# Two buffers for key-query loads, shifted keys and the middle block, kept sums in DRAM, and attention pairs traced four steps apart

## The chip, the cores and the metric

The kernel runs on one core of a Trainium2 chip. The metric is the device time of one execution in microseconds (us); lower is better. The core's engines are TensorE (PE, with its weight loads as PEld), VectorE (DVE), ScalarE (ACT), GpSimd (POOL) and SyncE (SP), which here only issues DMAs. Each engine works through its own list of instructions in order.

## The reference

```python
def phi(x):
    proj = np.einsum('bhsd,df->bhsf', x, w_phi)
    proj = proj - np.max(np.abs(proj), axis=-1, keepdims=True)
    return np.concatenate([np.exp(proj), np.exp(-proj)], axis=-1)
q_p, k_p = (phi(q), phi(k))                       # batch 4, heads 8, seq 576, head_dim 64, 128 features
kv = np.einsum('bhsf,bhsd->bhfd', k_p, v)
z = np.sum(k_p, axis=2)
num = np.einsum('bhsf,bhfd->bhsd', q_p, kv)
den = np.einsum('bhsf,bhf->bhs', q_p, z)[..., None] + 1e-06
x = num / den                                     # reshaped to 2304 tokens x 512
h = x @ w_in                                      # 512 x 2048, weights given in 64 bits
g = np.where(h > 0.0, h, np.exp(np.minimum(h, 0.0)) - 1.0)
x = g @ w_out                                     # 2048 x 512
for e in range(4):                                # second layer: 4 experts of 512 x 1024 x 512
    out += p[:, e:e + 1] * (np.maximum(x @ w1[e], 0.0) @ w2[e])
```

## The kernel before

The work has three stages that overlap in the order in which the engines get it.

**Attention.** The 32 heads are worked on two at a time: 16 pairs, each a Python generator `pair(i)`. One pair does the following. It projects keys and queries with `w_phi` (L209 for the middle block of 64 keys and 64 queries, L192 sixteen times: eight for the keys, eight for the queries). DVE takes the largest absolute value of each row (L198) and subtracts it (L199, into `md`, `kp` and `qd`). ACT exponentiates the shifted keys (L202, L203). PE transposes the shifted queries (L238, L256), and ACT exponentiates them on their way out of PSUM (L246, into `ew`). PE multiplies keys with values (L231, L232: the keys are the stationary operand, the values the moving one), where the tile `vt` holds 64 columns of values and 64 columns of ones, so that the sum over keys comes out with the product. ACT copies that product out of PSUM (L260, `kvw`). PE then computes the denominator (L295) and the numerator (L285) from `kvw` and `ew`. The reciprocal goes through DRAM to be spread over partitions (L309, L313), DVE multiplies (L316), and ACT and POOL split the result into two parts `xh` and `xl`, the input of the next stage.

**First layer ("Elu").** 2304 tokens are 9 tiles of 256; the hidden dimension's first half is 4 units `u`. `Elu.l1` makes 24 matmuls (L483 to L485) of 128x256, `Elu.l2` makes 24 more (L512 to L514), two units later. The first two tiles are done in two halves (`SEG`), so their sum after unit 1 is kept until unit 3 (`drain`). The weights arrive as 64-bit words and are converted by `convert64`: a DMA (L108), two ACT steps (L116, L117), four DVE steps (L120 to L123), POOL steps (L125, L127), and a split (L132, L134). `CVL` is how many conversions are loaded ahead of the `CVB` = 4 that are being worked on; the pool has `CVB + CVL` buffers for them.

**The rest**, from about 455 us on, is the second half of the first layer and the four experts, in a Strassen form (L610 to L612, L712 to L714).

Attention is traced step by step: `attention()` starts a new pair every `ATT_LAG` steps and advances each live pair by one yield per step. The Elu units are traced between, and a scheduler in the compiler then orders all instructions of all engines by its own model, so that the constants below act through the order it finds. `load(i + 1)` issues a pair's loads of keys, queries and values; `kq` has `LDB` buffers, `vt` two by hand.

Of the kernel before, what the change touches and what calls it, by code (L numbers as in the profile page):

```python
# [8 lines left out]
F32 = mybir.dt.float32  # L9
# [4 lines left out]
ALU = mybir.AluOpType  # L14
# [3 lines left out]
B, H, S, D, FEAT = 4, 8, 576, 64, 128  # L18
NT, DM, DFF, E, F2 = 2304, 512, 2048, 4, 1024
P = 128  # L20
KD = DM // P
NP = H // 2
HS = S // 2
Q = 32
TS = 256
# [15 lines left out]
WL = 'G'  # L41
LAG = 2
RING = 16
ATT_LAG = 5
PRE = 1.2
RATE = 1.4
WRATE = 2
WHEAD = 5
CVB = 4
CVL = 2  # L50
TAIL = 2
HEAD = 2
SEG = 2
# [3 lines left out]
CB = 2  # L57
TEB = 2
PB = 4
LDB = 1  # L60
CVP = 16
CVW = 256
CVOFF = 0
# [5 lines left out]
def attn_elu_moe_kernel(ctx: ExitStack, tc: tile.TileContext, kq_in, vv, w_phi, w_in, w_out, probs, w1, w2, out):  # L69
    nc = tc.nc  # L70
    V, A, G, PE, SP = nc.vector, nc.scalar, nc.gpsimd, nc.tensor, nc.sync
# [5 lines left out]
    def pool(name, bufs=1, stack=ctx, **kw):  # L77
        return stack.enter_context(tc.tile_pool(name=name, bufs=bufs, reuse_waits="tile", **kw))

    const = pool("const")  # L80
    dram = ctx.enter_context(tc.tile_pool(name="dram", bufs=1, space=bass.MemoryType.DRAM))
# [4 lines left out]
    xvd = [[dram.tile([P, 2, 2, TC], F32, name=f"xvd{g}_{k}") for k in range(7)] for g in range(NG)]  # L86
    rscr = [dram.tile([2, S], F32, name=f"rec{i}") for i in range(B * NP)]
    x1scr = [dram.tile([P, KD, TS], F32, name=f"x1scr{t}") for t in range(NTS)]
    ring = pool("ring", RING)
    pst = ExitStack()  # L90
    psum = [pool("psum", 7, space=PSUM, stack=pst)]
# [14 lines left out]
    def convert64(dst, src, adder):  # L106
        st = cv.tile([P, CVW], I64, tag="w64", name="w64", bufs=CVB + CVL)
        SP.dma_start(st, src)  # L108
# [29 lines left out]
    tmp = pool("tmp", stack=right, side="right")  # L138
    gt = pool("gt", LAG + 1, stack=right, side="right")
    ld = pool("ld", LDB, stack=att)  # L140
    a1 = pool("a1", stack=att)
    wbd = a1.tile([P, 2, FEAT], F32, name="wbd")
    ident = a1.tile([P, P], F32, name="ident")
    vt = []

    def load(i):
        b, p = divmod(i, NP)
        kq = ld.tile([P, 2 * S], F32, tag="kq", name="kq")
        SP.dma_start(kq[:, :640], kq_in[b, p, :, :640])
        if i == 0:  # L150
            SP.dma_start(wbd, w_phi)
        SP.dma_start(kq[:, 640:], kq_in[b, p, :, 640:])
        v = vt[i % 2]
        SP.dma_start(v[:, 0:4, 0:D], vv[b, p, :, 0:4, :])
        SP.dma_start(v[:, 4:8, D:P], vv[b, p, :, 4:8, :])
        SP.dma_start(v[0:D, 8, 0:D], vv[b, p, 0:D, 8, :])
        SP.dma_start(v[0:D, 9, D:P], vv[b, p, D:P, 8, :])
        return kq, v

    def bank(shape=(P, 512)):  # L160
        return psum[0].tile(list(shape), F32, tag="bank", name="bank")
# [7 lines left out]

    make_identity(nc, ident)  # L170
    for i in range(2):
        t = a1.tile([P, 10, P], F32, name=f"vt{i}")
        G.memset(t, 1.0)
        vt.append(t)
    kpm = a1.tile([P, 2, 2, P], F32, name="kpm")
    G.memset(kpm, 0.0)
    loaded = {0: load(0)}

    def blocks(t, n):
        return t[:, :n * P].rearrange("p (n f) -> p n f", f=P)  # L180

    def pair(i):
        b, p = divmod(i, NP)
        kq, v = loaded.pop(i)
        kt, qt = kq[:, :512], kq[:, 640:]

        def proj(src):
            ps = [bank() for _ in range(2)]
            for t in range(4):
                for h in range(2):  # L190
                    r = slice(h * D, h * D + D)
                    PE.matmul(blocks(ps[h], 4)[:, t], src[r, t * P:(t + 1) * P], wbd[r, h], start=True, stop=True)  # L192
            return ps

        def guard(dst, ps, n):
            src = blocks(ps, n)
            mx = a1.tile([P, n, 1], F32, tag=f"mx{n}", name="mx", bufs=2)
            V.tensor_reduce(out=mx[:, :, 0], in_=src, op=ALU.max, axis=AX.X, apply_absolute_value=True)  # L198
            mark[0] = V.tensor_tensor(out=dst, in0=src, in1=mx.to_broadcast([P, n, P]), op=ALU.subtract).ins  # L199

        def kexp(d0, d1, src):
            A.activation(d0, src, ACTF.Exp)  # L202
            A.activation(d1, src, ACTF.Exp, scale=-1.0)  # L203

        kp = [a1.tile([P, 4, 2, P], F32, tag=f"kp{j}", name=f"kp{j}") for j in range(2)]
        md = a1.tile([P, 2, P], F32, tag="md", name="md")
        qd = [a1.tile([P, 4, P], F32, tag=f"qd{j}", name=f"qd{j}") for j in range(2)]
        pm = bank()
        PE.matmul(pm[:, :2 * FEAT], kq[:, 512:640], wbd, start=True, stop=True)  # L209
# [7 lines left out]
        yield  # L217
        kexp(kpm[:D, :, 0], kpm[:D, :, 1], md[:D])
        kexp(kp[1][:, :, 0], kp[1][:, :, 1], kp[1][:, :, 1])
        pq0, pq1 = proj(qt)  # L220
        guard(qd[0], pq0, 4)
        if i + 1 < B * NP:
            loaded[i + 1] = load(i + 1)
        yield
        guard(qd[1], pq1, 4)
        yield
        pk = bank((P, 4, P))

        def kv(h, c):
            for t in range(4):  # L230
# [3 lines left out]
        def tpose(j):  # L234
            pt = bank()
            for t in range(2):
                for h in range(2):
                    PE.transpose(blocks(pt, 4)[:, 2 * h + t], qd[h][:, 2 * j + t], ident)  # L238
            return pt

        ew = a1.tile([P, 2, 2, S], F32, tag=("eh", "el")[i % 2], name="ew")

        def qexp(ps, c0, n):
            src = ps[:, :512].rearrange("p (h s) -> p h s", h=2)[:, :, :n] if n > P else blocks(ps, 2)[:, :, P - n:]
            for c, sc in ((0, 1.0), (1, -1.0)):
                A.activation(ew[:, :, c, c0:c0 + n], src, ACTF.Exp, scale=sc)  # L246

        kvw = a1.tile([P, 4, P], F32, tag=("kvh", "kvl")[i % 2], name="kvw")
        qexp(tpose(0), 0, 256)
        kv(0, 0)  # L250
        kv(0, 1)
# [25 lines left out]
        def half(s):  # L277
            return slice(s * HS, (s + 1) * HS)

        def num(s):  # L280
            pn = bank()
            for c in range(2):
                for h in range(2):
                    r = slice(h * D, h * D + D)
                    PE.matmul(pn[r, :HS], kvw[:, 2 * h + c, r], ew[:, h, c, half(s)], start=(c == 0), stop=(c == 1))  # L285
            A.activation(nd[:, half(s)], pn[:, :HS], ACTF.Copy)

        def den():
            pd = bank()
            for c in range(2):  # L290
                for h in range(2):
                    for s in range(2):
                        g = (2 * h + s) * Q
                        ones = D - h * D
                        PE.matmul(pd[g:g + Q, :HS], kvw[:, 2 * h + c, ones:ones + Q], ew[:, h, c, half(s)], start=(c == 0), stop=(c == 1))  # L295
            A.activation(dd, pd[:, :HS], ACTF.Copy)

        dd = a1.tile([P, HS], F32, tag="dd", name="dd")
# [20 lines left out]
    done = [0]  # L319

    def attention():
# [3 lines left out]
        while nxt < B * NP or live:  # L325
            if nxt < B * NP and step % ATT_LAG == 0:
                live.append(pair(nxt))
# [62 lines left out]
    def weight_stream():  # L390
# [3 lines left out]
        while more or loaded or live:  # L394
            if more and len(loaded) < CVL:
                g = next(todo, "end")
                if g == "end":
                    more = False
                else:
                    next(g[0])  # L400
                    loaded.append(g)
            if loaded and len(live) < CVB and (len(loaded) == CVL or not more):
                live.append(loaded.pop(0))
# [59 lines left out]
            next(weights, None)  # L463

    stream = attention()
    accs, saved = {}, {}
    HU = FP // 2
    count = [0]

    class Elu:  # L470
# [28 lines left out]

        def l2(self, slot):  # L500
            key = self.t
            if self.first:
                accs[key] = [bank((P, 2, TS)) for a in range(2)]
            acc = accs[key]
            for j in range(2):
                w = rings["out", 2 * self.u + j]
                for dc in range(KD):
                    c = slice(dc * P, (dc + 1) * P)
                    o = acc[dc // 2][:, dc % 2]
                    start = self.first and j == 0 and dc % 2 == 0  # L510
                    stop = self.last and j == 1 and dc % 2 == 1
                    PE.matmul(o, w[:, 0, c], self.gh[:, j], start=start, stop=False)  # L512
                    PE.matmul(o, w[:, 0, c], self.gl[:, j], start=False, stop=False)  # L513
                    PE.matmul(o, w[:, 1, c], self.gh[:, j], start=False, stop=stop)  # L514
                if j == 0:
                    slot()
            if self.last:
                self.drain(acc)
            if self.t == NTS - 1:
                release(("out", 2 * self.u), ("out", 2 * self.u + 1))  # L520
            slot()

        def drain(self, acc):
            done = self.u == HU - 1
            for a in range(2):
                st = (tmp if done else a1).tile([P, 2, TS], F32, tag="xs" if done else "xp", name="xs", bufs=2 if done else 2 * HEAD)
                if (self.t, a) in saved:
                    V.tensor_tensor(out=st, in0=acc[a], in1=saved[self.t, a], op=ALU.add)
                else:
                    A.activation(st, acc[a], ACTF.Copy)  # L530
                if done:
                    A.dma_start(x1scr[self.t][:, 2 * a:2 * a + 2], st)
                else:
                    saved[self.t, a] = st

    def pieces(i, size):
        o = 0
# [426 lines left out]
```

## Time and profile before

| | |
|---|---|
| median of three runs | 1411.74 us (1411.62 to 1415.79) |
| the profiled execution, its device time | 1409.39 us |
| span of the profiled execution, first to last instruction | 1407.6 us |
| PE busy | 1361.3 us, 97% of the span |
| DVE, ACT, POOL busy | 664.9, 601.5, 361.1 us |
| mean granted TensorE clock | 0.992 of full speed |

Busy time is the union of an engine's instructions; what is left of the span is idle. The granted clock is the share of TensorE's clock that it was given: 1.00 is 2.4 GHz, 0.50 is 1.2 GHz. PE is busy nearly all the time, so the question for any stage is when PE waits there, and for whom.

### The profile page before, as it was taken

The numbers are of one execution on the slowest core, as the hardware profiler recorded it, in microseconds if no ns is written. First come the engines' busy times: TensorE is split into PE (matmuls) and PEld (weight loads), VectorE is DVE, ScalarE is ACT, GpSimd is POOL, SyncE is SP. The second block draws the span as 40 slices with busy tenths as digits, with TensorE's granted clock in tenths as the row PEclk, the third lists the DMA queues.
The fourth block names the chain that finished last, engine by engine and source line by source line (L and its number), as shares of the span: only waits on it lengthen the run. The fifth ranks groups of instructions, "written<-read, shape, count | busy, mean of one in ns | idle before, by whom it ended". The sixth has DMA issues, their size and how long they took to land.

```text
span 1407.6 us, 22023 instructions
## 1 busy us (share of the span) xinstructions
PE 1361.3 (97%) x8408; PEld 1234.4 (88%) x8408; DVE 664.9 (47%) x1212; ACT 601.5 (43%) x1347; POOL 361.1 (26%) x433
## 2 busy tenths in 40 slices
PE   6799899999999999999999999999999999999998
PEld 6678778888999899999898989888888989889897
DVE  5677766564443666684433423324433325323232
ACT  5667755554545646573333442123421214321121
POOL 3457644221226211263202440002420004300000
PEclk9999989999999999999999999999999999999999
DMA  5434455431324130446425142434145351433521
GB/s 160 135 121 143 130 178 157 138 111 46 116 78 128 42 118 29 128 167 208 155 92 207 37 156 91 157 115 148 53 150 209 103 175 45 142 120 128 179 68 68
DMA packets 105337, 173.46 MB, mean 123 GB/s; under 512 B 33040, under 2 KB 50576, under 8 KB 105232
## 3 DMA queue, kind: packets, MB, share of 16 engines
q1 hardware_dynamic: 98224, 162.55, 35.5%
q10 hardware_dynamic: 7008, 9.51, 1.9%
q8 instruction: 66, 1.08, 0.3%
q14 instruction: 39, 0.32, 0.1%
HBM read 118.13 MB, written 53.81 MB: 122 GB/s over the span
## 4 chain that ended last, share of the span: by engine, by line
PE 69%; DMA 5%; issue 3%; POOL 3%; DVE 3%; ACT 2%; SPq 0%; ACTq 0%; DVEq 0%; POOLq 0%
PE bank L610 9%; PE bank L612 9%; PE bank L611 9%; PE bank L712 9%; PE bank L713 9%; PE bank L714 9%; PE bank L689 2%; PE bank L690 2%; PE bank L691 2%; DMA w<-in_w_out 2%; POOL w L443 1%; DMA wst<-in_w 1%; PE bank L483 1%; PE bank L512 1%; PE bank L485 1%
## 5 line engine op out<-in xcount | busy, mean ns | idle before, releaser
L610 PE MATMUL bank<-xv,w 128*128 128x384 f32 x840 | 278.5, 336 | 4.8 <-DVE c L661 2.6
L611 PE MATMUL bank<-xv,w 128*128 128x384 f32 x840 | 281.8, 335 | 0.0
L612 PE MATMUL bank<-xv,w 128*128 128x384 f32 x840 | 277.8, 335 | 0.0
L713 PE MATMUL bank<-w,h 128*128 128x512 f32 x576 | 227.4, 395 | 0.0
L712 PE MATMUL bank<-w,h 128*128 128x512 f32 x576 | 225.7, 395 | 1.0 <-ACT h L626 0.9
L714 PE MATMUL bank<-w,h 128*128 128x512 f32 x576 | 202.8, 396 | 0.0
L443 POOL TENSOR_TENSOR w<-wst,w 128x256 fp32r<-128x256 f32 x100 | 78.1, 801 | 370.2 <-ACT w L442 360.7
L610 PEld LDWEIGHTS bank<-xv,w 128*128 128x128 f32 x840 | 157.6, 188 | 13.7 <-DVE c L661 3.2
L611 PEld LDWEIGHTS bank<-xv,w 128*128 128x128 f32 x840 | 157.7, 188 | 4.8
L612 PEld LDWEIGHTS bank<-xv,w 128*128 128x128 f32 x840 | 157.3, 188 | 0.0
L627 DVE SCALAR_TENSOR_TENSOR h<-bank,h 128x384 fp32r<-128x384 f32 x144 | 77.2, 554 | 124.7 <-ACT h L626 124.7
L626 ACT ACTIVATE h<-bank 128x384 fp32r<-128x384 f32 x144 | 66.7, 489 | 149.3 <-PE bank L612 93.3
L712 PEld LDWEIGHTS bank<-w,h 128*128 128x128 f32 x576 | 108.2, 188 | 23.7 <-ACT h L626 1.7
L713 PEld LDWEIGHTS bank<-w,h 128*128 128x128 f32 x576 | 108.2, 188 | 23.0
L714 PEld LDWEIGHTS bank<-w,h 128*128 128x128 f32 x576 | 107.2, 188 | 21.8 <-DVE h L627 1.0
L616 ACT ACTIVATE cmab<-bank 128x384 f32<-128x384 f32 x60 | 29.4, 491 | 191.9 <-PE bank L612 191.9
L561 POOL TENSOR_TENSOR xv<-xs,xv 128x768 fp32r<-128x768 f32 x24 | 45.8, 1910 | 190.9 <-ACT xv L560 182.2
L483 PE MATMUL bank<-xh,w 128*128 128x256 f32 x288 | 84.2, 292 | 3.2 <-ACT w L132 1.6
L512 PE MATMUL bank<-gh,w 128*128 128x256 f32 x288 | 84.6, 294 | 0.0
L484 PE MATMUL bank<-xl,w 128*128 128x256 f32 x288 | 81.5, 283 | 0.3 <-POOL xl L272 0.3
L624 DVE TENSOR_TENSOR c<-cmab,bank 128x384 f32<-128x384 f32 x48 | 26.6, 554 | 116.6 <-ACT cmab L616 116.6
L513 PE MATMUL bank<-gl,w 128*128 128x256 f32 x288 | 81.4, 283 | 0.0
(110 smaller groups left out, 2596.9 us busy)
## 6 DMA issues: line engine op xcount, KB each, us to landing
xv<-xvd SPq DMA_DIRECT2D x42, 768.0 KB, 5.1
wst<-in_w SPq DMA_DIRECT2D x64, 256.0 KB, 2.8
xvd<-xv SPq DMA_DIRECT2D x21, 768.0 KB, 4.8
yscr<-y SPq DMA_DIRECT2D x54, 256.0 KB, 2.0
y<-yscr SPq DMA_DIRECT2D x54, 256.0 KB, 3.3
w<-in_w_in SPq DMA_DIRECT2D x32, 256.0 KB, 3.3
w<-in_w_out SPq DMA_DIRECT2D x32, 256.0 KB, 2.9
kq<-in_kq SPq DMA_DIRECT2D x16, 320.0 KB, 3.4
```

The lines of the kernel that those rows point to most:

```text
L443: on[WL[v % len(WL)]].tensor_tensor(out=lo, in0=x, in1=f32(hi), op=ALU.subtract)
L483: PE.matmul(ph[:, j], w[:, 0, c], xh[:, kc], start=(kc == j == 0), stop=False)
L484: PE.matmul(ph[:, j], w[:, 0, c], xl[:, kc], start=False, stop=False)
L512: PE.matmul(o, w[:, 0, c], self.gh[:, j], start=start, stop=False)
L513: PE.matmul(o, w[:, 0, c], self.gl[:, j], start=False, stop=False)
L610: PE.matmul(o, hi[:, c], x[:, 0, kc], start=not more and kc == 0, stop=False, skip_group_check=more)
L611: PE.matmul(o, hi[:, c], x[:, 1, kc], start=False, stop=False, skip_group_check=more)
L612: PE.matmul(o, lo[:, c], x[:, 0, kc], start=False, stop=kc == 1, skip_group_check=more)
L627: V.scalar_tensor_tensor(out=h[:, 1], in0=c, scalar=0.0, in1=f32(h[:, 0]), op0=ALU.max, op1=ALU.subtract)
L712: PE.matmul(self.acc, h[:, 0, c], w[:, 0], start=f == 0, stop=False)
L713: PE.matmul(self.acc, h[:, 0, c], w[:, 1], start=False, stop=False)
L714: PE.matmul(self.acc, h[:, 1, c], w[:, 0], start=False, stop=f == 2 * NQ - 1)
```

## The change

The constants `ATT_LAG` (5 to 4), `CVL` (2 to 1) and `LDB` (1 to 2) change. The tiles `kp` (shifted keys and their exponentials) and `md` (the middle block) get two buffers instead of one. The next pair's loads are traced ahead of the query projection instead of behind it. The values tile and the key-value product have 64 + 32 columns a block instead of 64 + 64 (one block of ones suffices for both heads), so that the key-value matmuls stream 96 columns instead of 128, and the values of full blocks come in one DMA instead of two. The sums of the first two Elu tiles after unit 1 are written to DRAM (`x1head`) and read back ahead of unit 3, instead of being kept in SBUF.

```diff
-ATT_LAG = 5
+ATT_LAG = 4
-CVL = 2
+CVL = 1
-LDB = 1
+LDB = 2
...
+    x1head = [dram.tile([P, KD, TS], F32, name=f"x1head{t}") for t in range(HEAD)]
...
-        SP.dma_start(v[:, 0:4, 0:D], vv[b, p, :, 0:4, :])
-        SP.dma_start(v[:, 4:8, D:P], vv[b, p, :, 4:8, :])
+        SP.dma_start(v[:, 0:8, 0:D], vv[b, p, :, 0:8, :])
...
-        t = a1.tile([P, 10, P], F32, name=f"vt{i}")
+        t = a1.tile([P, 10, D + Q], F32, name=f"vt{i}")
...
-        kp = [a1.tile([P, 4, 2, P], F32, tag=f"kp{j}", name=f"kp{j}") for j in range(2)]
-        md = a1.tile([P, 2, P], F32, tag="md", name="md")
+        kp = [a1.tile([P, 4, 2, P], F32, tag=f"kp{j}", name=f"kp{j}", bufs=2) for j in range(2)]
+        md = a1.tile([P, 2, P], F32, tag="md", name="md", bufs=2)
...
+        if i + 1 < B * NP:
+            loaded[i + 1] = load(i + 1)
         pq0, pq1 = proj(qt)
         guard(qd[0], pq0, 4)
-        if i + 1 < B * NP:
-            loaded[i + 1] = load(i + 1)
...
-        pk = bank((P, 4, P))
+        pk = bank((P, 4, D + Q))
...
-        kvw = a1.tile([P, 4, P], F32, tag=("kvh", "kvl")[i % 2], name="kvw")
+        kvw = a1.tile([P, 4, D + Q], F32, tag=("kvh", "kvl")[i % 2], name="kvw")
...
-                        PE.matmul(pd[g:g + Q, :HS], kvw[:, 2 * h + c, ones:ones + Q], ew[:, h, c, half(s)], start=(c == 0), stop=(c == 1))
+                        PE.matmul(pd[g:g + Q, :HS], kvw[:, 2 * h + c, D:], ew[:, h, c, half(s)], start=(c == 0), stop=(c == 1))
...
+            self.kept = []
+            if self.t < HEAD and self.u == HU - 1:
+                for a in range(2):
+                    st = tmp.tile([P, 2, TS], F32, tag="xs", name="xs", bufs=2)
+                    SP.dma_start(st, x1head[self.t][:, 2 * a:2 * a + 2])
+                    self.kept.append(st)
...
-                st = (tmp if done else a1).tile([P, 2, TS], F32, tag="xs" if done else "xp", name="xs", bufs=2 if done else 2 * HEAD)
-                if (self.t, a) in saved:
-                    V.tensor_tensor(out=st, in0=acc[a], in1=saved[self.t, a], op=ALU.add)
+                if self.kept:
+                    st = self.kept[a]
+                    V.tensor_tensor(out=st, in0=acc[a], in1=st, op=ALU.add)
                 else:
+                    st = tmp.tile([P, 2, TS], F32, tag="xs", name="xs", bufs=2)
                     A.activation(st, acc[a], ACTF.Copy)
-                if done:
-                    A.dma_start(x1scr[self.t][:, 2 * a:2 * a + 2], st)
-                else:
-                    saved[self.t, a] = st
+                A.dma_start(to[:, half], st)
```

The order of instructions moves in three places that matter here. The line numbers of the changed kernel differ by one to five from those of before (L295 is L294 there, L117 is L118, L132 is L133). Elsewhere the order is nearly kept: from the first experts' work on, every engine has the same rows.

**First place: PE in the head of the program**, where attention alone runs; the end of the second pair's key-value product (L231, L232), its denominator and numerator (L295 or L294, L285) and the third pair's first transpose (L238 of `qd_465`, now `qd_428`). Before:

```order
L192 MATMUL bank<-wbd,kq 128x128 x8
L295 MATMUL bank<-ew,kvw 32x288 x8
L285 MATMUL bank<-ew,kvw 64x288 x8
L192 MATMUL bank<-wbd,kq 128x128 x8
L238 MATMUL bank<-ident,qd_465 128x128
L231 MATMUL bank<-vt_184,kp_462 128x128 x4
L232 MATMUL bank<-vt_184,kpm 128x128
```

and now:

```order
L232 MATMUL bank<-vt_188,kpm 128x96
L294 MATMUL bank<-ew,kvw 32x288 x8
L192 MATMUL bank<-wbd,kq 128x128 x8
L285 MATMUL bank<-ew,kvw 64x288 x8
L209 MATMUL bank<-wbd,kq 128x256
L238 MATMUL bank<-ident,qd_428 128x128
L231 MATMUL bank<-vt_186,kp_425 128x96 x4
L232 MATMUL bank<-vt_186,kpm 128x96
```

The first eight L192 (the third pair's keys) have moved up, to between the two halves of the second pair's key-value product, so that the denominator now follows that product directly. The other eight (the third pair's queries) no longer stand just ahead of the transposes of the same queries: the numerator and an L209 stand between.

**Second place: ACT at the same point**, from the exponentials of the second pair's middle block (`kpm`) to the copy of its key-value product (L260). Before:

```order
L202 ACTIVATE kpm<-md 64x2x128
L269 ACTIVATE xh<-nd 128x256
L271 DMA xscr_60<-nd 128x576
L269 ACTIVATE xh<-nd 128x256
L269 ACTIVATE xh<-nd 128x64
L260 ACTIVATE kvw<-bank 128x512
```

and now:

```order
L202 ACTIVATE kpm<-md 64x2x128
L202 ACTIVATE kp_425<-kp_425 128x4x128
L118 ACTIVATE w_695<-w_695 128x256
L202 ACTIVATE kp_426<-kp_426 128x4x128
L203 ACTIVATE kp_425<-kp_425 128x4x128
L260 ACTIVATE kvw<-bank 128x384
```

Ahead of the copy there stood the split of the first pair's result (L269); now three exponentials of the third pair's keys and a conversion step stand there, and the split has moved behind.

**Third place: PE in the stretch in which attention and Elu units mix**, where the ninth pair's queries are projected and transposed. Before:

```order
L514 MATMUL bank<-gh,w 128x256
L192 MATMUL bank<-wbd,kq 128x128 x8
L238 MATMUL bank<-ident,qd_2114 128x128
L231 MATMUL bank<-vt_184,kp_2111 128x128 x4
L232 MATMUL bank<-vt_184,kpm 128x128
```

and now, where the eight L192 stand twelve rows of Elu matmuls ahead of the first of these rows:

```order
L285 MATMUL bank<-ew,kvw 64x288 x8
L209 MATMUL bank<-wbd,kq 128x256
L519 MATMUL bank<-gh,w 128x256
L517 MATMUL bank<-gh,w 128x256
L518 MATMUL bank<-gl,w 128x256
L519 MATMUL bank<-gh,w 128x256
L238 MATMUL bank<-ident,qd_1970 128x128
```

The transposes followed the projection directly; now twelve Elu matmuls, the numerator, an L209 and four more Elu matmuls lie between.

## Rows read from the trace of the kernel before

**Rows 1.** Busy time by stage: stretch, length, busy time and instructions, clock, DMA.

```profile
0.00:85.40 85.40, 64.49 (x551) 53.99 (x551) 51.80 (x114) 50.41 (x128) 32.45 (x53) 0.94 0.48 145
85.40:315.00 229.60, 217.08 (x1892) 190.09 (x1891) 157.45 (x347) 142.57 (x357) 115.53 (x163) 0.98 0.46 141
315.00:455.00 140.00, 140.00 (x1184) 133.56 (x1183) 61.48 (x99) 72.43 (x148) 43.08 (x49) 1.00 0.29 90
```

**Rows 2.** Waits of PE, whole program: us in total, times, longest.

```profile
PE bank L238 <- DVE qd L199: 13.8, 4, 5.5
PE bank L295 <- ACT kvw L260: 5.7, 6, 1.8
PE bank L238 <- DVE dn L307: 4.1, 2, 2.1
...
PE bank L483 <- ACT w L132: 1.6, 1, 1.6
```

**Rows 3.** Busy time in short stretches (columns as in rows 1).

```profile
27.10:29.10 2.00, 0.00 (x0) 0.00 (x0) 1.99 (x5) 1.85 (x5) 1.09 (x3) 1.00 0.43 123
29.10:36.40 7.30, 7.26 (x68) 6.89 (x68) 4.43 (x11) 3.68 (x10) 2.74 (x4) 1.00 0.60 178
42.60:44.70 2.10, 0.05 (x1) 0.08 (x1) 2.08 (x4) 1.49 (x4) 1.50 (x3) 1.00 0.44 114
44.80:48.20 3.40, 3.40 (x17) 3.40 (x17) 2.23 (x7) 0.73 (x2) 0.98 (x3) 0.50 0.49 171
58.70:60.80 2.10, 0.04 (x2) 0.02 (x1) 2.03 (x4) 1.37 (x4) 1.13 (x2) 1.00 0.45 95
174.50:181.30 6.80, 3.73 (x18) 3.74 (x19) 6.28 (x16) 1.55 (x4) 3.16 (x5) 0.50 0.86 272
```

**Rows 4.** Timeline, 35 to 45 us: start, length, engine, line, tiles, idle before.

```profile
35.25 1.16 PE L192 MATMUL bank<-wbd,kq 64*128 64x128 f32 x16
...
37.59 0.58 ACT L260 ACTIVATE kvw<-bank 128x512 f32<-128x512 f32 x1
...
38.23 1.18 PE L295 MATMUL bank<-ew,kvw 128*32 128x288 f32 x16 [1.81 <-ACT kvw L260]
...
39.33 2.16 PE L285 MATMUL bank<-ew,kvw 128*64 128x288 f32 x16
...
39.78 0.62 ACT L202 ACTIVATE kp<-kp 128x512 f32<-128x512 f32 x1
...
42.62 1.29 DVE L198 TENSOR_REDUCE mx<-bank 128x4 f32<-128x512 f32 x2 [1.20 <-PE bank L192]
...
43.82 0.68 DVE L199 TENSOR_TENSOR qd<-bank,mx 128x512 f32<-128x512 f32 x1
...
44.65 0.36 PE L238 MATMUL bank<-ident,qd 128*128 128x128 f32 x1 [2.06 <-DVE qd L199]
```

**Rows 5.** One run of key-value matmuls in the timeline.

```profile
30.39 1.06 PE L231 MATMUL bank<-vt,kp 128*128 128x128 f32 x8
```

**Rows 6.** Groups by line and shape: records, busy us, mean ns (first four 195 to 315 us, last two 0 to 470).

```profile
L231 PEld LDWEIGHTS bank<-vt,kp 128*128 128x128 f32 x160 | 19.7, 192 | 0.0
L285 PEld LDWEIGHTS bank<-ew,kvw 128*64 128x64 f32 x80 | 5.3, 136 | 3.6
L295 PEld LDWEIGHTS bank<-ew,kvw 128*32 128x32 f32 x64 | 1.7, 109 | 3.2 <-ACT kvw L260 2.2
...
L231 PE MATMUL bank<-vt,kp 128*128 128x128 f32 x160 | 21.6, 275 | 0.0
...
L231 PE MATMUL bank<-vt,kp 128*128 128x128 f32 x512 | 75.6, 293 | 0.0
L232 PE MATMUL bank<-vt,kpm 128*128 128x128 f32 x128 | 26.4, 290 | 0.0
```

**Rows 7.** Weight conversions: their splits from 85 to 163 us, and SP's waits.

```profile
L132 ACT ACTIVATE w<-top x21: 402/417/464, 85.1 to 161.1; 128x256 fp32r<-128x256 f32 x21
...
SPq L108 <- POOL top L127: 38.4, 20, 4.0
```

More of the change, by code (lines that the diff above doesn't have):

```diff
@@ L153, in load @@
         v = vt[i % 2]
-        SP.dma_start(v[:, 0:4, 0:D], vv[b, p, :, 0:4, :])
-        SP.dma_start(v[:, 4:8, D:P], vv[b, p, :, 4:8, :])
+        SP.dma_start(v[:, 0:8, 0:D], vv[b, p, :, 0:8, :])
         SP.dma_start(v[0:D, 8, 0:D], vv[b, p, 0:D, 8, :])
-        SP.dma_start(v[0:D, 9, D:P], vv[b, p, D:P, 8, :])
+        SP.dma_start(v[0:D, 9, 0:D], vv[b, p, D:P, 8, :])
         return kq, v
@@ L284, in num @@
                     r = slice(h * D, h * D + D)
-                    PE.matmul(pn[r, :HS], kvw[:, 2 * h + c, r], ew[:, h, c, half(s)], start=(c == 0), stop=(c == 1))
+                    PE.matmul(pn[r, :HS], kvw[:, 2 * h + c, :D], ew[:, h, c, half(s)], start=(c == 0), stop=(c == 1))
             A.activation(nd[:, half(s)], pn[:, :HS], ACTF.Copy)
@@ L293, in den @@
                         g = (2 * h + s) * Q
-                        ones = D - h * D
-                        PE.matmul(pd[g:g + Q, :HS], kvw[:, 2 * h + c, ones:ones + Q], ew[:, h, c, half(s)], start=(c == 0), stop=(c == 1))
+                        PE.matmul(pd[g:g + Q, :HS], kvw[:, 2 * h + c, D:], ew[:, h, c, half(s)], start=(c == 0), stop=(c == 1))
             A.activation(dd, pd[:, :HS], ACTF.Copy)
@@ L465, in attn_elu_moe_kernel @@
     stream = attention()
-    accs, saved = {}, {}
+    accs = {}
     HU = FP // 2
@@ L523, in drain @@
         def drain(self, acc):
-            done = self.u == HU - 1
+            to = x1scr[self.t] if self.u == HU - 1 else x1head[self.t]
             for a in range(2):
-                st = (tmp if done else a1).tile([P, 2, TS], F32, tag="xs" if done else "xp", name="xs", bufs=2 if done else 2 * HEAD)
-                if (self.t, a) in saved:
-                    V.tensor_tensor(out=st, in0=acc[a], in1=saved[self.t, a], op=ALU.add)
+                half = slice(2 * a, 2 * a + 2)
+                if self.kept:
+                    st = self.kept[a]
+                    V.tensor_tensor(out=st, in0=acc[a], in1=st, op=ALU.add)
                 else:
+                    st = tmp.tile([P, 2, TS], F32, tag="xs", name="xs", bufs=2)
                     A.activation(st, acc[a], ACTF.Copy)
-                if done:
-                    A.dma_start(x1scr[self.t][:, 2 * a:2 * a + 2], st)
-                else:
-                    saved[self.t, a] = st
+                A.dma_start(to[:, half], st)
     def pieces(i, size):
```

## The prediction

> **What bounds the kernel now.** I first split the span by stage. In the head, where attention runs alone, PE is busy 64.49 of 85.40 us; while attention and Elu units mix, 217.08 of 229.60; from 315 to 455 us all of it [rows 1]. So the change, all of which lies in attention and the Elu stage, can win only where PE idles (20.9 and 12.5 us), where its clock is low, or by giving PE less to do. After 455 us the order is nearly the same on every engine, and I expect nothing there.
>
> Next, who ends PE's waits. Two hand-overs carry most of it: the transposes (L238) wait for the shifted queries from DVE, 13.8 us in four waits and 4.1 in two more that are put down to DVE's next instruction; the denominator (L295) waits for ACT's copy of the key-value product, 5.7 us in six [rows 2]. The timeline shows why: the query projection ends near 42.6 us, the two reductions take 1.29 us, the subtraction 0.68, and only then, after 2.06 us of idle time, can the transposes start; nothing else stood between on PE [rows 4]. Near 37 us the copy on ACT comes late and the denominator waits 1.81 us [rows 4].
>
> The clock is the last view. After the gap at 42.6 us the granted clock is 0.50 (1.2 of 2.4 GHz) from 44.8 to 48.2 us, but after the equally long gap at 27.1 us it stays at 1.00 [rows 3]. So a gap of 2 us sometimes costs half of another 3.4 us, 1.7 us. The whole head cycle from one such gap to the next (42.6 to 58.7 us) is 16.1 us [rows 3].
>
> **The change, part by part.**
>
> *Order in the head (two buffers for `kp`, `md`, `kq`; `ATT_LAG` 4).* Between the query projection and the transposes there now stand the numerator (2.16 us) and an L209. Reductions and subtraction need 1.29 + 0.68, about 2.0 us [rows 4], so the 2.06 us wait goes; since DVE also has conversion steps in its list there, of about the size of ACT's 0.417 us [rows 7], I leave 0.4 us of it. But the denominator has lost its cover: it stood behind eight L192 (1.16 us, rows 4), and now directly follows the key-value product. And on ACT the copy stands behind three exponentials of the next pair's keys. From the end of that pair's key projection the chain is: reductions 1.29, two subtractions of 0.68, the exponential of the second half 0.62, that of the first half again 0.62, the copy 0.5 (0.58 times 96/128, with some overhead), a conversion step of 0.42 between: 4.7 us [rows 4, 7]. PE covers this with six transposes and twenty key-value records, at 0.112 us each (next part) 2.9 us. So a wait of about 1.8 us (1.4 without the conversion step, 2.0, which I take, with hand-over) comes back at the denominator in each head cycle. A cycle before: 16.1 us, with 2.06 for the transposes, 0.95 for the denominator (5.7 over six, rows 2) and 1.7 of clock, hence 11.4 of work. A cycle now: 11.4 + 0.4 + 2.0 = 13.8, and 15.5 if the clock still falls each time. I take the clock loss in half the cycles: 14.7, a gain of 1.4 in each of four cycles. The first cycle loses: its key projection (1.16) and one exponential (0.62) now stand ahead of the first denominator. Head: 4 x 1.4 - 1.8, about 4 us; bounds -1 (clock always low, worse wait) and +9 (clock never low).
>
> *Order in the mixed stretch.* Its losses are 12.5 us idle [rows 1] and low clock: of 174.5 to 181.3 us PE worked 3.73 us at half speed, 1.9 us lost [rows 3]. The longest wait, 5.5 us, is that of the ninth pair's transposes [rows 2], which followed their projection directly and now have sixteen Elu matmuls, the numerator and an L209 ahead of them: more than 4 us of cover. I leave 1 us. Against that, in the new order the ninth denominator has no cover (2 us), two more have little (0.6 each), the wait of L483 for its weights (1.6, rows 2) stays, and some 1.5 us of small waits stay: 7.3 us. I let the clock fall once in two cases (0.9). So 14.4 lost becomes 8.2: 6 us gained; bounds 0 and 12.
>
> *96 instead of 128 columns.* There are 512 + 128 records of key-value matmuls [rows 6], two for each instruction. Eight of them in a row take 1.06 us, and one alone 0.275 [rows 6], so they start (1.06 - 0.275)/7 = 0.112 us apart [rows 5]. If that distance went with the moving columns it would fall by a quarter, 28 ns, and 640 records would give 17.9 us. But a record also loads 128 columns of weights, whose number does not change. The weight loads' mean durations are 109, 136 and 192 ns for 32, 64 and 128 columns: 27 ns for 32 columns more and 56 ns for 64 more, 0.85 to 0.88 ns a column [rows 6]. At that slope 128 columns hold the weight path for about 110 ns, which is the distance seen. So I take almost nothing, 1 us; bounds 0 and 17.9.
>
> The Trainium skill, TensorE: Matmul & The Clock Gate, section LDWEIGHTS (loading the stationary operand), says that a weight load takes time by its columns alone, columns / 1.2 ns, whatever the rows; that is 107 ns for 128 columns, in agreement with the slope above. It speaks against this part of the change: by it the distance could fall from 112 to 107 ns at most, an estimated 3 us over 640 records.
>
> *`CVL` 1.* One buffer fewer for 64-bit weights. The number of conversions that ACT has behind it when each pair's product is copied is the same in both orders within one, so I cost it at nothing; the cover is that the buffer removed held a load that was only waiting. Without the cover it is the last rival below.
>
> *Kept sums in DRAM, one DMA fewer for values, later releases.* Four more DMA issues on ACT and four loads on SP, well ahead of their additions, and 16 DMAs fewer on SP. What is behind the loads on SP are conversion loads and key-query loads, and the latter now have a second buffer, so a wait there is covered; 0, bound 2 us lost.
>
> Sum: 4 + 6 + 1 = 11 us. The profiled execution took 1409.39 us, its span 1407.6; the median of the runs is 1411.74, 2.3 above, and I subtract from it: 1401 us.
>
> **The rivals.**
>
> *The narrower matmuls pay in full.* If the distance goes with moving columns, 10 + 17.9, about 28 us: 1384. For it: nothing on the trace shows the weight path alone setting a distance, as no group pairs 128 weight columns with a shorter stream. Against it: the slope. The Trainium skill's same page, section Back-to-back issue gap, gives columns / 2.4 + 2.5 ns for an isolated stream, which would leave 82 ns for 192 column-steps, and says that in real streams weight load and matmul set the distance together.
>
> *The wait only moves.* The denominator's wait of 2 us takes the place of the transposes' wait, the clock falls after each as it did at 44.8 us, and in the mixed stretch ACT and DVE, 62% to 69% busy there [rows 1], give new waits as fast as old ones go. Head 0, stretch 1, columns 1: 1410. For it: ACT's list ahead of the copy is longer than before, not shorter.
>
> *Slower: the conversions fall behind.* From 85.1 to 161.1 us twenty intervals pass, 3.8 us each [rows 7]. With six buffers a load's residence is at most 6 x 3.8 = 22.8 us, and SP did wait for a buffer (38.4 us in twenty waits, rows 7). If the residence does not shrink when a buffer goes, five of them give 4.6 us each, twenty take 15.2 us longer, and the first tiles' units 2 and 3, one of which already waited 1.6 us for weights [rows 2], wait for nearly all of it. With 4 of the head and 5 of the later stretch still won: 1411.74 + 15.2 - 9 = 1418. It decides once conversions take over 4.3 us each. Against it: PE waited only once, 1.6 us, for weights, and loads that stand ready need no extra buffer.
>
> **How the numbers follow.** The forecast's mechanism (waits at the transposes gone, shorter ones at the denominator left) gets 0.53, and its own range is 1393 to 1409; the full gain of narrow columns 0.13; the moved wait 0.19; the slow conversions 0.12; 0.03 for what I have not thought of. A change under 0.3% (4.2 us, so 1407.5 to 1416) cannot be told from none here. Faster: 0.13 and nearly all of 0.53, with some of the moved wait: 0.69. Same: most of 0.19 and the edges of its neighbours: 0.20. Slower: 0.11. The range leaves about 1 in 10 on each side: 1383 to 1414.
>
> **What would show it.** Right, if PE's waits of L238 for `qd` fall from 13.8 us to under 4, the denominator's waits for `kvw` grow (now L294) from 5.7 us to some 10 or more, the stretch with Elu units loses fewer than 10 us, and the key-value records still start 0.107 to 0.112 us apart. The columns' part is wrong if these records start 0.085 us apart. The conversions' part is wrong if L482 waits for weights for several us or the splits between the 12th and 32nd conversion come over 4.3 us apart. The head is wrong if the clock stays at 0.50 after every denominator, or never.

## The result and the profile after

The changed kernel takes 1430.55 us (median of 4 runs, 1426.09 to 1433.09), beside 1412.47 us (4 runs, 1411.62 to 1415.79) for the kernel before on the same chip: ratio 1.0135, 95% interval 1.0112 to 1.0158. It is slower by some 18 us where 11 us of gain were forecast. The profiled execution took 1426.09 us with a span of 1424.3, 16.7 more than before.

Busy time by stage in the changed kernel, columns as in [rows 1]; the first stage ends where the first Elu matmul starts, now at 92.4 us:

```profile
0.00:92.40 92.40, 68.79 (x583) 53.72 (x583) 54.14 (x120) 54.69 (x139) 33.92 (x56) 0.92 0.47 144
92.40:315.00 222.60, 202.43 (x1725) 176.33 (x1722) 142.68 (x319) 128.60 (x323) 106.09 (x152) 0.95 0.48 144
315.00:455.00 140.00, 140.00 (x1193) 131.91 (x1193) 66.84 (x111) 72.62 (x152) 38.73 (x46) 1.00 0.25 77
```

PE idles for 23.6 us in the head and 20.2 in the mixed stretch, 43.8 together; before it was 20.9 + 12.5 = 33.4 [rows 1]. The clock is lower too. Length times missing clock is 92.4 x 0.08 + 222.6 x 0.05 = 18.5 us now, and 85.4 x 0.06 + 229.6 x 0.02 = 9.7 before. So 10.4 us of idle time and 8.8 of clock came on top, which is the 16.7 of the span and a little more.

PE's waits, as in [rows 2]:

```profile
PE bank L294 <- ACT kvw L260: 34.4, 10, 6.0
...
PE bank L238 <- DVE qd L199: 1.9, 1, 1.9
...
PE bank L517 <- ACT w L133: 1.5, 1, 1.5
...
PE bank L209 <- DMA kq<-in_kq: 1.0, 1, 1.0
```

The transposes hardly wait now (13.8 + 4.1 us before), but the denominator waits for the copy of the key-value product six times as long (5.7 us before): 3.00 us in the first pair, 13.6 in the next four, and 17.8 in five waits of the mixed stretch. The timeline of the second pair shows the reason; POOL, SP, ACT and PE rows are put in order of time:

```profile
33.11 0.74 POOL L128 TENSOR_TENSOR top<-top,w 128x256 f32<-128x256 f32 x1
33.69 1.19 SPq L312 DMA_DIRECT2D rb<-rec  x2
34.98 0.53 SPq L109 DMA_DIRECT2D w<-in_w_in  x1
35.92 1.06 PE L231 MATMUL bank<-vt,kp 128*128 128x96 f32 x8
36.44 0.61 ACT L202 ACTIVATE kp<-kp 128x512 f32<-128x512 f32 x1
36.81 0.39 PE L232 MATMUL bank<-vt,kpm 128*128 128x96 f32 x2
39.95 0.43 ACT L118 ACTIVATE w<-w 128x256 f32<-128x256 uint32 x1 [2.89 <-DMA w<-in_w_in]
40.28 0.61 ACT L202 ACTIVATE kp<-kp 128x512 f32<-128x512 f32 x1
40.80 0.61 ACT L203 ACTIVATE kp<-kp 128x512 f32<-128x512 f32 x1
41.32 0.47 ACT L260 ACTIVATE kvw<-bank 128x384 f32<-128x384 f32 x1
41.84 2.15 PE L294 MATMUL bank<-ew,kvw 128*32 128x288 f32 x16 [4.64 <-ACT kvw L260]
```

The product is done at 37.20 us. On ACT the conversion step L118 stands ahead of two exponentials and of the copy, and its 64-bit words have not landed: ACT stands still for 2.89 us with work behind it that is ready (DVE had the last of the shifted keys done at 37.04). The load was issued at 34.98, right behind the reload of the reciprocals (L312), and the step could start 4.97 us later. In the next three pairs the same step waits 1.29, 0.82 and 1.44 us, and the denominator 3.11, 2.61 and 3.19. Taken off, the load's wait leaves 1.75, 1.82, 1.79 and 1.75 us. In the mixed stretch the step mostly stands further ahead of the copy on ACT (it waits 2.64 us up to 139.55, and the copy starts at 146.91), so the load's part of those waits can't be read off row by row.

The Trainium skill, PSUM — Partial Sum Buffer, section Engine vs sequencer instructions, calls ScalarE's queue a strict first-in, first-out one; the row of L118 agrees.

Over the whole program ACT waits for these loads about as long as before, so the sum of its waits tells nothing; the place does. Changed kernel:

```profile
ACT w L118 <- DMA w<-in_w_in: 35.5, 22, 3.0
ACT w L118 <- DMA w<-in_w_out: 31.7, 16, 5.5
```

Before (L117 there):

```profile
ACT w L117 <- DMA w<-in_w_out: 47.0, 21, 4.7
ACT w L117 <- DMA w<-in_w_in: 27.8, 17, 3.3
```

### The profile page after: what moved, and what is told of

Read it like the earlier page. It is cut to its first block, busy times and chain, and to the rows that moved or that the text cites. A ratio compares the mean times of both kernels' runs of the same rounds, so it can differ in the third digit from the quotient of the medians.

```text
span 1424.3 us, 22004 instructions
## 1 busy us (share of the span) xinstructions
PE 1368.3 (96%) x8408; PEld 1236.3 (87%) x8408; DVE 664.7 (47%) x1212; ACT 602.3 (42%) x1347; POOL 360.6 (25%) x433
## 4 chain that ended last, share of the span: by engine, by line
PE 76%; DMA 2%; issue 2%; DVE 1%; ACT 1%; POOL 1%; DVEq 0%; POOLq 0%; ACTq 0%
PE bank L614 9%; PE bank L616 9%; PE bank L615 9%; PE bank L716 9%; PE bank L717 9%; PE bank L718 9%; PE bank L693 2%; PE bank L694 2%; PE bank L695 2%; PE bank L482 2%; PE bank L484 2%; PE bank L518 2%; PE bank L483 2%; PE bank L517 2%; PE bank L519 2%
## 5 line engine op out<-in xcount | busy, mean ns | idle before, releaser
L482 PE MATMUL bank<-xh,w 128*128 128x256 f32 x288 | 87.7, 305 | 0.0
L517 PE MATMUL bank<-gh,w 128*128 128x256 f32 x288 | 83.2, 290 | 1.9 <-ACT w L133 1.5
L484 PE MATMUL bank<-xh,w 128*128 128x256 f32 x288 | 83.2, 289 | 0.0
```

What stands on the lines that cost most here:

```text
L482: PE.matmul(ph[:, j], w[:, 0, c], xh[:, kc], start=(kc == j == 0), stop=False)
L484: PE.matmul(ph[:, j], w[:, 1, c], xh[:, kc], start=False, stop=(kc == KD - 1 and j == 1))
```

## The experiments

Theory A: in the four-step order the denominator has lost its cover on PE, and on ACT a step that waits for a load stands ahead of its copy. Theory B: the conversions are late because of the buffer that `CVL` 1 took away, in whatever order. Each run is compared with the kernel before on its own chip (medians 1409.0 to 1414.5 us).

**Parts of the change, alone or undone.** Changed kernel with five steps:

```diff
-ATT_LAG = 4
+ATT_LAG = 5
```

> The changed kernel with pairs started every five steps again, all else as changed. In its order eight L192 stand between the key-value product and the denominator again, and no exponential of the next pair ahead of the product's copy. Theory A (the four-step order costs the time: denominator without cover, its copy on ACT behind the next pair's exponentials and a conversion step that waits for its load): 1403 to 1414 us, waits of the denominator for the copy under 8 us instead of 34.4, waits of the transposes back near 18 us. Theory B (one load-ahead buffer fewer makes ACT wait for conversion loads, whatever the order): stays at 1425 or above.

1413.62 us, ratio 1.0014 (0.9996 to 1.0032): all 17 us come back. PE's waits are again those of before:

```profile
PE bank L238 <- DVE qd L199: 11.9, 3, 5.8
PE bank L238 <- DVE dn L306: 6.2, 3, 2.1
PE bank L294 <- ACT kvw L260: 5.5, 3, 2.9
```

So the four steps do the harm; the rest of the change together is worth nothing that the interval can tell. Kernel before with one conversion buffer fewer:

```diff
-CVL = 2
+CVL = 1
```

> The kernel before with CVL 1 alone. Theory A: within 4 us of before, 1408 to 1416. Theory B: 1420 or more, with ACT's waits for conversion loads well over the 75 us that they took before.

1415.58 us, 1.0026 (1.001 to 1.0042): a small loss, far from 18. Kernel before with four steps:

```diff
-ATT_LAG = 5
+ATT_LAG = 4
```

> The kernel before with ATT_LAG 4 alone, single buffers, two loads ahead. In its order the denominator follows the key-value product directly, but only one exponential of the next pair and no conversion step stand ahead of the copy in the first five pairs. Theory A: slower than before, 1416 to 1428, with denominator waits of 15 to 30 us and fewer waits of the transposes. Theory B: 1408 to 1416.

1423.07 us, 1.0074 (1.0045 to 1.0103). Slower as theory A says, but by another wait than expected: with one `kq` buffer L209 waits 17.0 us for keys and queries, and the denominator only 10.3, under the 15 to 30 expected:

```profile
PE bank L209 <- DMA kq<-in_kq: 17.0, 6, 6.2
PE bank L295 <- ACT kvw L260: 10.3, 6, 4.7
```

So this run does not bear theory A's mechanism out. Kernel before with the narrow values alone (and one values DMA fewer):

```diff
-        t = a1.tile([P, 10, P], F32, name=f"vt{i}")
+        t = a1.tile([P, 10, D + Q], F32, name=f"vt{i}")
...
-        pk = bank((P, 4, P))
+        pk = bank((P, 4, D + Q))
```

> The kernel before with the narrow values and product alone (96 columns instead of 128, one values DMA fewer), five steps, single buffers. If the weight load of 128 columns sets the distance of these matmuls: their starts stay 0.110 to 0.112 us apart and the time within 3 us of before. If the columns set it: 0.085 us apart and some 10 us or more faster.

1417.77 us, 1.0044 (1.0026 to 1.0063). The narrower stream wins nothing. PE is idle exactly as long as before, 17.7 + 15.7 = 33.4 us, but its clock in the head is 0.84 where it was 0.94 [rows 1]:

```profile
0.00:87.60 87.60, 69.85 (x551) 59.01 (x551) 50.39 (x111) 49.49 (x127) 32.64 (x54) 0.84 0.46 139
87.60:315.00 227.40, 211.71 (x1831) 185.26 (x1831) 157.23 (x344) 137.53 (x346) 113.00 (x159) 0.97 0.46 138
```

**What stands ahead of the copy.** Changed kernel with the low word's scaling on GpSimd:

```diff
-        A.activation(f32(lo), lo, ACTF.Copy, scale=2.0 ** -52)
+        G.tensor_scalar(out=f32(lo), in0=lo, scalar1=2.0 ** -52, scalar2=None, op0=ALU.mult)
```

> The changed kernel with the conversion's scaling of the low words (L118) moved from ACT to GpSimd, so that ACT's list no longer has an instruction that waits for a conversion load except where the Abs step comes first. The order of PE is nearly that of the changed kernel, the denominator still without cover. If the load's wait on ACT makes the denominator's wait longer than forecast (2.9, 1.3, 0.8 and 1.4 us of it in pairs two to five): those four waits fall from 13.6 us to about 6, the denominator's waits in all from 34 to 15 to 22, time 1414 to 1422. If the exponentials alone set it: waits stay above 28 us and the time at 1425 or more.

1413.46 us, 1.0007 (0.9989 to 1.0025): 17 us back, and the denominator's waits fall from 34.4 to 20.5 us. But the wait for the load now stands on POOL:

```profile
POOL w L118 <- DMA w<-in_w_out: 42.0, 18, 5.2
```

The same edit in the kernel before:

> The kernel before with the scaling step on GpSimd instead of ACT. If ACT's wait for the conversion load costs only where the step stands ahead of the copy that the uncovered denominator waits for (the four-step order): within 4 us of before, 1408 to 1415. If it costs ACT time in any order: 8 us or more faster, 1403 or less.

1412.87 us, 1.0009 (0.9995 to 1.0023): nothing. Changed kernel with one buffer for `kp` and `md`, which changes what ACT has ahead of the copy:

```diff
-        kp = [a1.tile([P, 4, 2, P], F32, tag=f"kp{j}", name=f"kp{j}", bufs=2) for j in range(2)]
-        md = a1.tile([P, 2, P], F32, tag="md", name="md", bufs=2)
+        kp = [a1.tile([P, 4, 2, P], F32, tag=f"kp{j}", name=f"kp{j}") for j in range(2)]
+        md = a1.tile([P, 2, P], F32, tag="md", name="md")
```

> The changed kernel with single buffers for the shifted keys and the middle block; two for the loads, four steps, CVL 1. In its order the denominator is as uncovered as in the changed kernel, but ahead of the copy stands mostly one exponential, and a conversion step in one of the first five pairs instead of four. If what stands ahead of the copy on ACT sets the wait: denominator waits in the first five pairs 5 to 9 us instead of 16.6, time 1410 to 1420. If the missing cover alone sets it: 1425 or more.

1418.53 us, 1.0046 (1.0027 to 1.0065), denominator's waits 14.3 us: 12 of the 18 us back. Both of these edits together:

> The changed kernel with one buffer for the shifted keys and the middle block, and the low word's scaling on GpSimd: both things taken away that stood ahead of the copy. Theory A: the parts that each gave alone (12 and 17 us) overlap, so about 1410 to 1415, the denominator's waits under 15 us. If they are separate costs and add up: 1402 to 1407, which would beat both kernels.

1415.55 us, 1.0023 (1.0006 to 1.004). They do not add up; the denominator's waits are 14.1 us, and L482 now waits 8.8 us for converted weights. Changed kernel with the copy on DVE:

```diff
-        A.activation(kvw, pk, ACTF.Copy)
+        V.tensor_copy(kvw, pk)
```

> The changed kernel with the copy of the key-value product on DVE, so that no load's wait on ACT stands ahead of it; DVE's list has the next pair's reductions and subtractions there instead, 2 to 3 us. Theory A: the denominator's waits fall from 34.4 us to under 20, time 1411 to 1420, though ACT still waits for the same loads. If it is the loss of PE's cover alone and the engine of the copy does not matter: waits stay at 28 us or more and the time at 1424 or more.

1416.72 us, 1.0042 (1.0018 to 1.0066). The denominator waits 16.4 us for the copy (and 3.8 for ACT's exponentials), while ACT waits for the loads nearly as long as in the changed kernel (65.7 and 67.2 us): the copy is earlier without a change in the loads, as theory A has it.

**Why the load is late.** Changed kernel with these loads issued from GpSimd:

```diff
-        SP.dma_start(st, src)
+        G.dma_start(st, src)
```

> The changed kernel with the loads of the 64-bit weights issued from GpSimd's queue instead of SyncE's; the scaling step (L118) that waits for them stays on ACT ahead of the product's copy, buffers and CVL stay. If the load comes late because it stands on SyncE behind the DMAs of the reciprocals, which wait themselves: the step waits less, the denominator's waits fall from 34 to under 24 us, time 1412 to 1421. If it comes late because a buffer fewer lets it be issued later: no change, 1425 or more.

1426.74 us, 1.011 (1.0083 to 1.0137): the denominator's waits fall to 24.9 us, but the time hardly does; why not was not followed. Now the load is issued 0.30 us after POOL's step L128 frees a buffer, and in the second pair L118 still waits 1.14 us. For one more buffer room had to be made, so a control comes first (denominator's small tiles in the buffer of `rb`, one tag for the row maxima, `CVL` still 1):

> Control for the run after it: the changed kernel, still CVL 1, with the denominator's two small tiles laid into one buffer of the tag of rb and one tag of three buffers for the row maxima, which makes room. In pairs 2 to 5 the conversion step still stands ahead of the copy. Both theories: as the changed kernel within 5 us, 1425 to 1435, denominator's waits of 28 to 38 us.

1428.44 us, 1.0111 (1.0088 to 1.0134), waits 33.6 us: as the changed kernel. Then with the buffer:

```diff
-CVL = 1
+CVL = 2
```

> The control with CVL 2: four steps apart and both extra conversion buffers. Theory that the load waits for its buffer: the load is issued 3 us or more earlier, ACT's waits ahead of the copies in pairs 2 to 5 (2.9, 1.3, 0.8 and 1.4 us in the changed kernel) fall under 0.5 us each, the denominator's waits to some 20 us as with the scaling on GpSimd, time 1411 to 1419. Theory that the buffer costs nothing, as predicted: 1425 or more, waits of 28 us or more.

1427.52 us, 1.0112 (1.0089 to 1.0135), waits 31.7 us. The buffer is worth nothing here. I expected the load to be issued 3 us earlier; it was not, as SP has it behind the reload of the reciprocals, where it stood before:

```profile
33.41 1.10 SPq L312 DMA_DIRECT2D rb<-rec  x2
34.61 0.52 SPq L109 DMA_DIRECT2D w<-in_w_in  x1
```

So theory B falls: in this order the buffer is not it. The load's place on SP makes part of the wait (34.4 us to 24.9 with the load on GpSimd), but little of the time; what is left is the step's place on ACT. The test that keeps the work and takes away only the wait orders the scaling behind the same conversion's absolute value, which waits for DVE, so that its words have long landed:

```diff
-        A.activation(ps, f32(hi), ACTF.Abs)
-        A.activation(f32(lo), lo, ACTF.Copy, scale=2.0 ** -52)
+        first = A.activation(ps, f32(hi), ACTF.Abs).ins
+        with tc.issue_after(first):
+            A.activation(f32(lo), lo, ACTF.Copy, scale=2.0 ** -52)
```

> The changed kernel with the low word's scaling kept on ACT but ordered behind the same conversion's absolute value, which itself waits for DVE, so it no longer stands between the exponentials and the copy of the key-value product. If the wait for the load at the head of ACT's list is the cause: no waits of ACT for these loads between 20 and 90 us, the denominator's waits fall from 34.4 to some 20 us, time 1411 to 1419. If it was ACT's work (40 times 0.42 us and more) that mattered: 1424 or more.

1398.62 us, 0.9902 (0.9863 to 0.9941): 32 us under the changed kernel, with the same instructions on ACT. PE's order is nearly that of the changed kernel as well: up to 315 us, 2264 of its 2303 records match in order by line and shape, where the runs with the scaling or the loads on GpSimd keep 1872 and 1887. So this is the cleanest of the tests. The timeline of the second pair (lines one higher here):

```profile
37.85 0.42 ACT L203 ACTIVATE kpm<-md 64x256 f32<-64x256 f32 x1
38.17 1.26 ACT L203 ACTIVATE kp<-kp 128x512 f32<-128x512 f32 x2
39.34 0.61 ACT L204 ACTIVATE kp<-kp 128x512 f32<-128x512 f32 x1
39.86 0.47 ACT L261 ACTIVATE kvw<-bank 128x384 f32<-128x384 f32 x1
40.38 1.18 PE L295 MATMUL bank<-ew,kvw 128*32 128x288 f32 x16 [1.45 <-ACT kvw L261]
```

and PE's waits in that run:

```profile
PE bank L295 <- ACT kvw L261: 14.8, 8, 3.1
...
PE bank L239 <- DVE qd L200: 2.3, 1, 2.3
```

ACT has no wait for these loads left but one of 1.7 us. Of the denominator's waits 8.4 us are in the five head pairs (16.6 in the changed kernel) and 6.4 in the mixed stretch (17.8). The gain is more than expected, since the wait had cost elsewhere too, as the same edit in the kernel before shows:

> The kernel before with the low word's scaling ordered behind the same conversion's absolute value. If only the four-step order puts that step ahead of the copy: 1409 to 1415, as with the scaling on GpSimd in the five-step order (1412.9), so the change is worth 11 to 16 us once the wait is gone, near the forecast's 11. If the ordering alone made the run fast: 1396 to 1402, and the change is worth nothing.

1397.11 us, 0.9917 (0.9898 to 0.9937). The higher expectation fell: the five-step order gains as well, and between the two orders nothing is left that the intervals can tell. The stages of this run, and below them those of the four-step one:

```profile
0.00:86.00 86.00, 62.34 (x550) 50.06 (x551) 51.38 (x113) 49.08 (x124) 32.44 (x53) 0.92 0.46 143
86.00:315.00 229.00, 226.32 (x2006) 199.80 (x2005) 167.44 (x364) 151.24 (x373) 117.69 (x167) 0.99 0.47 145
```

```profile
0.00:81.50 81.50, 65.63 (x583) 53.01 (x583) 53.77 (x120) 52.38 (x134) 32.90 (x55) 0.94 0.54 161
81.50:315.00 233.50, 226.41 (x2000) 198.94 (x1997) 161.90 (x360) 146.77 (x365) 115.62 (x166) 0.99 0.50 149
```

Four steps save 23.7 - 15.9 = 7.8 us of idle time in the head and lose 7.1 - 2.7 = 4.4 in the mixed stretch. The lower rows also hold the 32 us: against the changed kernel, idle time falls from 43.8 to 23.0 us and the clock's loss, worked out as above, from 18.5 to 7.2.

**Cover for both hand-overs.** Four steps, but with the older pair first in each round:

```diff
-            for g in list(live):
+            for g in reversed(list(live)):
```

> Still four steps apart, but within a round the older pair goes first. The denominator then has eight L192 or more of PE between itself and the key-value product again, and almost nothing stands ahead of its copy on ACT; the transposes follow their query projection directly again in most pairs. Theory A (copy late behind a conversion step that waits for its load, and no PE work to cover it): the denominator's waits fall from 34.4 us to under 10, the transposes' waits come back to 10 to 16 us, time 1408 to 1416. Theory B (the conversions lag with one buffer fewer, wherever they stand): no better than the changed kernel, 1425 or more.

1403.63 us, 0.9938 (0.9919 to 0.9956). Better than expected, since the transposes' waits did not come back. I had read the order wrongly there: the projection that the transposes follow directly is that of the next pair's keys; their own queries are projected ahead of the denominator (rows of the fastest version below). With the scaling on GpSimd:

> The run before this one, with the low word's scaling on GpSimd. Theory A: with the copy no longer behind it, moving the scaling away is worth nothing, within 3 us of the run before this one. Theory B: it helps in any order, 6 us or more below it.

1395.03 us, 0.9891 (0.9863 to 0.9919): 8.6 us more, where theory A had said none, which suggests that late loads cost here too, wherever they stand on ACT. With the extra buffer instead (in the control's tiles, and with the conversions under way also advanced in reversed order):

> The older pair first in each round, with CVL 2. If the buffer matters only where a conversion step stands ahead of an uncovered denominator: within 4 us of the older-first run with CVL 1 (1403.6). If late loads cost by themselves wherever they stand on ACT: 6 us or more below it, near the older-first run with the scaling on GpSimd (1395.0).

1405.34 us, 0.9963 (0.9946 to 0.998), the denominator's waits 16.2 us where the older-first run has 11.6: no gain. As the conversions' order changed too, this does not single out the buffer. With the scaling ordered late:

> The same with the older pair first. If a wait for a load on ACT costs wherever it stands: 1393 to 1399, as with the scaling on GpSimd (1395.0). If the 8.6 us between the two older-first runs came from ACT's work being less: 1402 to 1407, as the older-first run with nothing else changed (1403.6).

1382.82 us, 0.9781 (0.9756 to 0.9806), the fastest version, below the expectation. Its PE rows in the head, and its first two stages:

```profile
36.57 1.16 PE L193 MATMUL bank<-wbd,kq 64*128 64x128 f32 x16
38.19 1.18 PE L295 MATMUL bank<-ew,kvw 128*32 128x288 f32 x16 [0.46 <-ACT kvw L261]
39.29 0.70 PE L210 MATMUL bank<-wbd,kq 128*128 128x256 f32 x2
39.92 2.16 PE L286 MATMUL bank<-ew,kvw 128*64 128x288 f32 x16
42.01 1.71 PE L193 MATMUL bank<-wbd,kq 64*128 64x128 f32 x16
43.65 0.66 PE L239 MATMUL bank<-ident,qd 128*128 128x128 f32 x4
```

```profile
0.00:79.00 79.00, 66.90 (x601) 53.14 (x601) 55.66 (x123) 53.42 (x135) 34.74 (x57) 0.98 0.57 165
79.00:315.00 236.00, 236.00 (x2117) 209.29 (x2116) 168.07 (x369) 161.17 (x385) 118.18 (x166) 1.00 0.50 151
```

The sixteen records of L193 at 36.57 (the queries' projection) stand between product and denominator; from there to the transposes stand the denominator, L210, the numerator and the next pair's keys. Both hand-overs have cover, and the mixed stretch has no idle time at all.

## Why the prediction was wrong

**The step that failed** is the chain ahead of the denominator's copy, where "a conversion step of 0.42 between" went in at the duration of its own row. That step opens with a wait for a load. Forecast were denominator waits of 4 x 2.0 = 8.0 us in the head and 3.2 in the mixed stretch, some 11; measured were 34.4, of them 13.6 in the same four head cycles and 17.8 in the mixed stretch. With the step ordered late they are 14.8. In the four head pairs the wait without the load's part is 1.75 to 1.82 us where the chain gave 1.8 (its terms as listed add up to 4.8 us, not 4.7), and with the step ordered late it is 1.45, 1.92, 1.32 and 1.45 where the chain without that step gave 1.4. In the head, the form of the chain was right; one link was read as work when it was work and a wait. In the mixed stretch the run with the step ordered late shows 11.4 us less of these waits, but not along which chain. The prediction took this chain from PE's waits and the durations of rows; ACT's own waits, 47.0 and 27.8 us for the same step before the change, went into no term.

**The clock** was to fall in half of the four head cycles, at 1.7 us each. It did fall to half after the second and the third pair's wait (4.64 and 3.11 us), stayed at 1.00 after the fourth's (2.61) and was at 0.65 from 91.0 to 94.5 us, after the fifth's (3.19). But each fall lasted twice as long as the one at 44.8 us before, so that PE worked 5.86 and 5.40 us in it and lost 2.9 and 2.7:

```profile
40.90:47.70 6.80, 5.86 (x40) 3.39 (x42) 3.25 (x7) 4.47 (x13) 4.46 (x7) 0.50 0.24 81
57.90:64.80 6.90, 5.40 (x38) 3.15 (x40) 1.96 (x6) 4.18 (x12) 3.72 (x6) 0.51 0.43 116
```

Up to 315 us the loss grew from 9.7 to 18.5 us, along with the longer waits. That the waits drew it down is likely, not shown: the narrow-values run lost 20.8 us, worked out alike, with no more idle time than before.

**The mixed stretch** was forecast to gain 6 us, and to lose fewer than 10 as a sign of being right; it idled 20.2 us and lost 11.1 to the clock. Even without the load's wait the four-step order idles 4.4 us longer there than the five-step one with the same cure; the head's 4 us were there, and more (7.8). So the forecast's 11 us would not have come with that wait away either: 1398.62 against 1397.11 us. The rival that the wait only moves comes nearest to this; that the new order as built is 17 us worse still is the load's wait.

**Right were** the transposes' waits (1.9 us, under the 4 of the forecast); the second `kq` buffer (1.0 us of waits, and 17.0 without it); the kept sums in DRAM and the narrow columns, worth nothing together in the five-step run. Eight key-value records still take 1.06 us, as [rows 5]; with 96 columns as with 128 they start 0.112 us apart. The Trainium skill, TensorE: Matmul & The Clock Gate, section LDWEIGHTS (loading the stationary operand), weighed in the prediction, gives columns / 1.2 ns for a load, an estimated 107 ns for 128 columns; the measured 112 ns agree within 5 ns. `CVL` 1 at nothing held in the four-step order; the run before with `CVL` 1 gives 0.26%.

**The slower rival** had the sign and not the cause. Its own condition did come about: the splits of the 12th to the 32nd conversion (L133, 85.0 to 174.4 us) are 4.47 us apart, over the 4.3 that the prediction named, where they were 3.8. But PE waited only 1.5 us for weights (L517); with the buffer given back in the four-step order they are 4.28 apart (4.44 in its control) and the time is the same; and with `CVL` 1 and the step ordered late they are 3.75 apart. So the conversions fell behind with the waits on ACT, not for want of a buffer.

What stays open: why GpSimd's scaling gained 17 us in the four-step order and none in the five-step one. POOL then waits for the loads in both, and what waits behind POOL was not followed. Nor was it why the loads issued from GpSimd cut the denominator's waits by 9.5 us and the time by only some 4, nor how much of each wait in the mixed stretch is a load's.

## What to carry to other kernels

An instruction that a new order puts ahead of a critical one costs its duration and its own wait, so look up what it waits for on that engine, not only who makes the bottleneck wait. A step that waits for a DMA belongs behind one that is bound to come late anyway: here 1398.6 for 1430.6 us in one order, and 0.8% in the other. A hand-over between engines is best judged by what the bottleneck has between producer and consumer: moving cover from one to another gained nothing, giving it to both took 1398.6 to 1382.8 us.

## What the runs showed of the hardware

The granted clock is no function of PE's idle time alone: with 33.4 us idle up to 315 us, the profiled execution of the kernel before ran its head at 0.94 and that of the narrow-values kernel at 0.84. A load of 256 KB took 4.97 us from its issue on SP to the start of the step that waits for it, and 4.06 us in the second pair of the run that issues it from GpSimd (36.32 to 40.38 us).
